# A 2-D Fourier mixer that adds x(t,e) and x(-t,-e) before its transforms instead of after them

## The chip, the cores and the metric

One core of a Trainium2 chip runs the whole kernel. The metric is the device time of one execution in microseconds, the median of the runs shown. The profile is of one execution; its times are microseconds from the start of its span. TensorE (PE) does the matmuls and the transposes, VectorE (DVE) and ScalarE (ACT) the elementwise work, GpSimd (POOL) next to nothing, and SyncE (SP) issues most of the DMAs.

## The reference

Two batches of 3136 tokens with 256 features go through an attention with squared ReLU, a low-rank token mixer with a first two-layer channel mixer, and then the stage that is changed here:

```python
def _moe2_ref(x, w_ch1, w_ch2) -> np.ndarray:
    X = np.fft.fft(x, axis=1)
    X = np.fft.fft(X, axis=2)
    mixed = np.real(X).astype(np.float32)
    u = x + mixed
    mu = np.mean(u, axis=-1, keepdims=True)
    var = np.mean((u - mu) ** 2, axis=-1, keepdims=True)
    un = (u - mu) / np.sqrt(var + 1e-06)
    ch = np.maximum(un @ w_ch1, 0.0) @ w_ch2
    return (u + ch).astype(np.float32)
```

The real part of the 2-D transform of x is what is wanted, for tokens (axis 1) and features (axis 2).

## The kernel before

The tokens are ordered so that the transform over 3136 = 64 x 49 tokens splits into one over 49 and one over 64, and so that negating a token index swaps neighbours (r) and moves whole stretches. Everything is float32; each factor of most matmuls is split into a high and a low part, so that a product is three matmuls.

After the attention comes one loop (the last of `program`) over the 28 chunks of the two channel mixers: two layers x two batches x seven chunks of 448 tokens. A chunk has eight hidden blocks, so the loop has 224 steps. Step i issues `hidden(i)` (six matmuls, then ReLU `Hh` on ScalarE, L323, and the low part `Hl` on VectorE, L324), then `project(i - 2)` (six matmuls into `psC`); the last project of a chunk ends in `finish` (two additions into `xT`, L353, in the first layer; two multiplications and two additions, L366 and L368, in the second). Then each generator in the list `active` issues one piece. `prep` of the next chunk is put at the head of the list at the third step of a chunk (k == 2); the others stand behind it in the order in which they were started: `tail` at step 3, `weights(0)` at 20, `fourier(0)` at 43, `fourier(1)` at 99, `weights(1)` at 104. The two Fourier generators rest at the first step of each chunk (k == 0). The schedule is manual: each engine gets its instructions in the order in which the program issues them, and waits are set where data need them.

`fourier(b)` works on `xT[b]`, which holds the features on the partitions (two halves, a = 0 and 1) and the tokens in the free dimension. `tokens(i)` transposes two stretches of 98 tokens, both halves, into one PSUM tile (four transposes, L768), and splits the result into `nh` (ScalarE) and `nl` (VectorE). `axis49(i - 1)` does the 49-point transform (three matmuls of 512 columns, L779 to L781), copies it to `wst` and stores it in DRAM (`scr`). That is 17 steps. `fetch` reads `scr` back, rearranged, as `wr`; after four steps `axis64` takes two of the 25 frequencies at a time, for each a matmul with both feature halves (L808), which yields the sums and differences of features e and -e. `features` then does the transform over the features (nine matmuls, L830 to L838) and adds its outputs to `xT` at both places. Feature 128 has no partner and is carried by a small side path (`er`, `feature128`, `row`).

`misc()` hands out three PSUM tiles (`m`, `x`, `g`) in turn. Helpers record their own line: ScalarE's copies are L92, VectorE's subtractions L95.

Of the kernel before, what the change touches and what calls it, by code (L numbers as in the profile page):

```python
# [10 lines left out]
F32 = mybir.dt.float32  # L11
# [16 lines left out]
def _orders():  # L28
    """Token order: position sl * 98 + i2 * 2 + r, with i1 = 2 * sl + r, holds the s with
    s = m1 (mod 64), s = m2 (mod 49), where m1 = o1[i1], m2 = o2[i2].  # L30

    o1 pairs each value with its negative, o2 runs 0..24, then -1..-24, so that a negation
    swaps r and moves whole stretches. Feature order: 0..127, then 128, -1, -2, .., -127.
    """
    o1 = np.array([0, 32] + [x for i in range(1, 32) for x in (i, 64 - i)])
    o2 = np.array(list(range(25)) + [49 - i for i in range(1, 25)])
    c1, c2 = pow(49, -1, 64), pow(64, -1, 49)
    tok = (49 * c1 * o1.reshape(32, 1, 2) + 64 * c2 * o2.reshape(1, 49, 1)) % S
    tok = tok.reshape(-1)
    feat = np.array(list(range(128)) + [128] + [256 - e for e in range(1, 128)])  # L40
    return o1, o2, c1, c2, tok, feat


def _constants():
    """DFT matrices (shapes alone): the 49-point and 64-point axes and the 256 features."""
    o1, o2, c1, c2, tok, feat = _orders()
    b49 = np.zeros((98, 128))
    t2 = 2 * np.pi * ((c2 * np.outer(o2, np.arange(KPOS))) % 49) / 49
    for par in range(2):
        b49[par::2, par * 32 : par * 32 + KPOS] = np.cos(t2)  # L50
        b49[par::2, 64 + par * 32 + 1 : 64 + par * 32 + KPOS] = np.sin(t2[:, 1:])
    t1 = 2 * np.pi * ((c1 * np.outer(o1, o1)) % 64) / 64
    f64 = np.block([[np.cos(t1), np.sin(t1)], [-np.sin(t1), np.cos(t1)]])
    row = np.array([2 * sl + par for par in range(2) for sl in range(32)])
    f64 = f64[np.concatenate([row, 64 + row])]
    e = np.arange(128)
    td = 2 * np.pi * (np.outer(e, e) % 256) / 256
    sign = np.zeros((128, 256))
    sign[:, 0] = 1.0 - 2.0 * (e % 2)
    sign[:2, 128:] = -2.0 * (e % 2)  # L60
    fd = np.concatenate([np.cos(td), np.sin(td), sign], axis=1)
    rep = np.tile(np.eye(32), (2, 4))
    mask = np.ones((128, 6))
    mask[:, 1] = mask[:, 2] = -1.0
    mask[0, :3] = [0.0, 0.0, 1.0]
    mask[:, 3] = 1e-6
    mask[:, 4] = -14336.0 * 2**19
    return {
        "b49": b49.astype(np.float32),
        "f64": f64.astype(np.float32),  # L70
        "fd": fd.astype(np.float32),
        "rep": rep.astype(np.float32),
        "mask": mask.astype(np.float32),
    }
# [7 lines left out]
def program(ctx, tc, zT, v, uT, U, V, w1a, w2a, w1b, w2b, b49, f64, fd, rep, mask, out):  # L82
# [34 lines left out]
    scr = [dram.tile([128, 32, D], F32, tag=f"scr{b}", name=f"scr{b}") for b in range(NB)]  # L117
# [4 lines left out]
    # constants  # L122
# [5 lines left out]
    f64s = [const.tile([128, 128], F32, name=f"f64s{a}") for a in range(2)]  # L128
# [3 lines left out]
    ones = const.tile([128, 128], F32R, name="ones")  # L132
    Utail = const.tile([128, 4, 64], F32R, name="Utail")
    Gs = [const.tile([128, D], F32R, name=f"Gs{b}") for b in range(NB)]

    def constants():
        make_identity(nc, ident)
        load(out=repc, in_=rep)
        load(out=maskc, in_=mask)
        t = ptile()  # L140
        load(out=t[0:98, 0:128], in_=b49)
        load(out=f64s[0], in_=f64)
        load(out=t[:, 256:768], in_=fd)
        nc.vector.memset(t[:, 768:896], 1.0 / D)
        yield
        yield
        hcopy(ones, t[:, 768:896])
        hcopy(b49h, t[0:98, 0:128])
        sub(b49l, t[0:98, 0:128], f(b49h))
        for dst, k in ((fA, 256), (fB, 384)):  # L150
            hcopy(dst[:, 0], t[:, k : k + 128])
            sub(dst[:, 1], t[:, k : k + 128], f(dst[:, 0]))
        hcopy(fN, t[:, 512:768].rearrange("p (a n) -> p a n", a=2))
        # the second half of the features: sines negated
        hcopy(f64s[1][:, 0:64], f64s[0][:, 0:64])
        nc.scalar.mul(f64s[1][:, 64:128], f64s[0][:, 64:128], -1.0)

    # float64 inputs arrive as their words
    def words(raw, np_, n):
        """float32 (the nearest) of the n float64 per partition at the start of raw."""  # L160
# [17 lines left out]
    # weights, in four tiles of 256 hidden units: [128, 2 (high, low), 2, 256], where the  # L178
    # third axis is the half of the features (first layer) or of the hidden units (second)
    class Weights:  # L180
# [3 lines left out]
        def split(self, k, y):  # L184
            """y: an eighth, [128, 256]"""
            part, q = divmod(k, 2)
            if q == 0:
                self.t[part] = self.pool.tile([128, 2, 2, 256], F32R, tag="w", name="w")
            w = self.t[part]
            if self.second:  # L190
                dst = w[:, :, q]
            else:
                y = y.rearrange("p (a n) -> p a n", a=2)
                dst = w[:, :, :, q * 128 : q * 128 + 128]
            hcopy(dst[:, 0], y)
            sub(dst[:, 1], y, f(dst[:, 0]))
# [15 lines left out]
    # the low-rank mixer: G = U^T a, accumulated over the tokens  # L212
# [11 lines left out]
    class Chunk:  # L224
# [33 lines left out]
        def prep2(self):  # L258
# [29 lines left out]
            # the variances: a row, then tokens 4 p + j on partition p  # L288
# [39 lines left out]
        def project(self, k):  # L328
# [5 lines left out]
            if self is chunks[-1] and k >= 6:  # L334
                # the first half of the features before the second, at the very end
# [38 lines left out]
    def attention(stack):  # L374
# [61 lines left out]
        # float64 inputs, piece by piece  # L436
# [31 lines left out]
        def conv_w(src, k, second, dst):  # L468
# [13 lines left out]
            if not second:  # L482
# [7 lines left out]
                # without its mean over the features: the norm's mean is gone with it  # L490
# [25 lines left out]
        def scores(b, qc, p):  # L516
# [13 lines left out]
            # the first one in halves: its products wait for it  # L530
# [33 lines left out]
        def gate(b, qc, last):  # L564
            """Two chunks share a tile: seven whole tiles of tokens for the mixer."""
# [11 lines left out]
        def groups(qc):  # L577
            """The tiles of 128 tokens (the last one has 64) that are worked on together."""
# [4 lines left out]
        def mix(b, qc, tiles, last):  # L583
            """The tiles' transposes."""
# [21 lines left out]
        def mix2(b, qc, tiles, h, l, n, last):  # L606
            """Their part of G."""
# [34 lines left out]
        # the engines' first instructions, before the data are there  # L642
# [116 lines left out]
    def fourier(b):  # L759
        """x <- x + Re(FFT2(x)) in place; yields between pieces of work."""  # L760
        nat, W = {}, {}

        def tokens(i):
            ps = misc()
            for s in range(2):
                for a in range(2):
                    src = xT[b][:, a, (2 * i + s) * 98 : (2 * i + s) * 98 + 98]
                    nc.tensor.transpose(  # L768
                        ps[0:98, s * D + a * 128 : s * D + a * 128 + 128], src, ident
                    )  # L770
# [5 lines left out]
        def axis49(i):  # L776
            h, l = nat.pop(i)
            ps = misc()
            mm(ps, b49h, h, start=True, stop=False)  # L779
            mm(ps, b49h, l, start=False, stop=False)  # L780
            mm(ps, b49l, h, start=False, stop=True)  # L781
            w = mp.tile([128, 512], F32, tag="wst", name="wst")
            hcopy(w, ps)
            load(out=scr[b][:, 2 * i : 2 * i + 2, :], in_=w.rearrange("p (s d) -> p s d", s=2))

        for i in range(17):
            if i < 16:
                tokens(i)
            if i > 0:
                axis49(i - 1)  # L790
            yield
# [3 lines left out]
        def fetch(g):  # L795
            n = min(2, KPOS - 2 * g)
            raw = W[g] = mp.tile([128, 2, D], F32, tag="wr", name="wr", bufs=3)
# [3 lines left out]
        def axis64(g, first, Th, Tl):  # L801
            """Two of the first 25 frequencies: the features' sums (cosine) and differences (sine)."""
# [3 lines left out]
            for j in range(n):  # L806
                for a in range(2):
                    mm(ps[:, j * 128 : j * 128 + 128], w[:, j, a * 128 : a * 128 + 128], f64s[a],  # L808
                       start=a == 0, stop=a == 1)
# [6 lines left out]
        # feature 128, which the folding of the features leaves on the wrong row  # L816
        e = mp.tile([128, KPOS], F32, tag="er", name="er", bufs=1)
        ch, cl = (mp.tile([KPOS, 64], F32R, tag=t, name=t, bufs=1) for t in ("ech", "ecl"))

        def feature128():  # L820
            ps = misc()
            mm(ps[0:KPOS, 0:64], e, f64s[0][:, 0:64], start=True, stop=True)
# [3 lines left out]
        def features(first, n, Th, Tl, row):  # L826
# [17 lines left out]
            # mneg is -1 except in row 0; sg is -1 except +1 in row 0  # L844
# [26 lines left out]
        for g in range(3):  # L871
            fetch(g)
            if g == 0:
                for c in range(4):
                    load(out=e[c * 32 : c * 32 + 32, :], in_=src[c, :, 0:KPOS, 128])
        for _ in range(4):
            yield
        late_adds = None
        for pairs in (range(0, 3), range(3, 6), range(6, 9), range(9, 13)):
# [3 lines left out]
            for g in pairs:  # L883
# [5 lines left out]
                if g == pairs[-1]:  # L889
                    # the high and the low part of feature 128, one row each  # L890
# [29 lines left out]
    with tc.manual_schedule():  # L920
# [3 lines left out]
            3: tail(), 20: weights(0), 43: fourier(0), 99: fourier(1), 13 * 8: weights(1),  # L924
        }
        calm = [starts[43], starts[99]]
# [31 lines left out]
def _host_layout(inputs):  # L958
# [15 lines left out]
    # the words of a float64 array, as the program reads them  # L974
# [23 lines left out]
```

## Time and profile before

| | |
|---|---|
| time, median of 3 runs | 1248.96 us (1248.58 to 1249.58) |
| span of the profiled execution | 1246.6 us |
| TensorE busy | 1239.5 us, 99% |
| VectorE busy | 814.2 us, 65% |
| ScalarE busy | 656.8 us, 53% |
| granted TensorE clock, mean | 1.000 |

The span runs from the first to the last instruction of the profiled execution. The profile has no separate total for that execution; the median of the runs is 2.4 us above the span, which is what lies around the instructions. The busy time of TensorE counts matmuls, whose ends are modelled and overlap. In the timeline rows a line is start, duration, engine, source line, operation, the tile written and the tiles read, and, in brackets, how long the engine had been idle and what it waited for.

### The profile page before, as it was taken

The page shows a single profiled execution, that of the slowest core. Times are in us where ns is not written, and L with a number is a line of the kernel's source. Part 1 is how long each engine was busy: PE and PEld are TensorE (multiplying, and loading weights), DVE is VectorE, ACT ScalarE, POOL GpSimd, SP SyncE. Part 2 cuts the span into 40 slices and gives each one's busy share as a digit, 9 for nine tenths or more (in the row PEclk, how much of TensorE's full clock was granted, in tenths as well). Part 3 has the DMA queues.
Part 4 walks back from the last instruction along what each step waited for, and adds up shares of the span by engine and source line. Part 5 has one row for each costly group of instructions (what it writes and reads, how often), then busy time and mean ns, then how long its engine had stood idle before and what let it go on. Part 6 is the DMA issues. An engine that isn't in the chain of part 4 may idle for free.

```text
span 1246.6 us, 16808 instructions
## 1 busy us (share of the span) xinstructions
PE 1239.5 (99%) x6270; PEld 1127.9 (90%) x6270; DVE 814.2 (65%) x1492; ACT 656.8 (53%) x1054; POOL 46.2 (4%) x90
## 2 busy tenths in 40 slices
PE   9999999999999999999999999999999999999998
PEld 7999999999899999999889988999989999999997
DVE  7867777988667566755555554567566677556564
ACT  7766676877566566666333354333465344343432
POOL 0000000000000000000000000000000111000100
PEclk9999999999999999999999999999999999999999
DMA  5311221334012112200221132321033221111111
GB/s 154 96 34 56 66 63 49 99 106 121 8 55 63 38 48 66 80 29 28 60 58 44 32 105 94 70 72 50 26 102 91 74 53 30 38 31 38 30 38 45
DMA packets 67297, 76.00 MB, mean 61 GB/s; under 512 B 18254, under 2 KB 60272, under 8 KB 67216
## 3 DMA queue, kind: packets, MB, share of 16 engines
q1 hardware_dynamic: 62752, 68.55, 18.3%
q0 software_dynamic: 4384, 6.27, 2.8%
q8 instruction: 49, 0.80, 0.3%
q14 instruction: 32, 0.26, 0.1%
q10 hardware_dynamic: 80, 0.11, 0.0%
HBM read 48.12 MB, written 23.76 MB: 58 GB/s over the span
## 4 chain that ended last, share of the span: by engine, by line
PE 96%; DVE 1%; ACT 1%; DMA 1%; issue 0%; SPq 0%; DVEq 0%; ACTq 0%
PE psO L560 11%; PE psO L557 11%; PE psO L559 11%; PE psH L318 7%; PE psC L343 7%; PE psC L345 7%; PE psH L319 7%; PE psC L344 7%; PE psH L320 7%; PE psS L527 6%; PE psS L528 6%; PE ps_g L612 1%; PE ps_m L593 1%; PE ps_m L808 1%; PE ps_x L808 1%; PE ps_g L808 1%
## 5 line engine op out<-in xcount | busy, mean ns | idle before, releaser
L324 DVE SCALAR_TENSOR_TENSOR Hl<-psH,Hh 128x448 fp32r<-128x448 f32 x224 | 139.7, 624 | 181.5 <-ACT Hh L323 181.4
L557 PE MATMUL psO<-h,Vt 128*128 128x448 f32 x700 | 256.5, 366 | 0.1
L560 PE MATMUL psO<-h,Vt 128*128 128x448 f32 x700 | 256.5, 366 | 0.0
L323 ACT ACTIVATE Hh<-psH 128x448 fp32r<-128x448 f32 x224 | 122.1, 545 | 245.2 <-PE psH L320 240.6
L559 PE MATMUL psO<-l,Vt 128*128 128x448 f32 x672 | 246.3, 366 | 0.4 <-DVE l L95 0.4
L533 ACT ACTIVATE P<-psS 128x896 f32<-128x896 f32 (+1 forms) x183 | 161.8, 885 | 149.1 <-PE psS L528 148.7
L95 DVE TENSOR_TENSOR l<-P,h 128x896 fp32r<-128x896 f32 (+1 forms) x197 | 201.2, 1021 | 23.5 <-ACT h L92 17.7
L537 DVE CAST h<-P 128x896 fp32r<-128x896 f32 (+1 forms) x183 | 111.0, 607 | 148.9 <-ACT P L536 147.6
L536 ACT ACTIVATE P<-P 128x896 f32<-128x896 f32 (+1 forms) x183 | 168.5, 921 | 5.7
L318 PE MATMUL psH<-h,w 128*128 128x448 f32 x448 | 166.6, 372 | 0.0
L319 PE MATMUL psH<-l,w 128*128 128x448 f32 x448 | 164.0, 366 | 0.2 <-DVE l L95 0.2
L343 PE MATMUL psC<-Hh,w 128*128 128x448 f32 x448 | 164.0, 366 | 0.0
L345 PE MATMUL psC<-Hh,w 128*128 128x448 f32 x448 | 163.9, 366 | 0.0
L344 PE MATMUL psC<-Hl,w 128*128 128x448 f32 x448 | 163.6, 365 | 0.0
L320 PE MATMUL psH<-h,w 128*128 128x448 f32 x448 | 163.4, 365 | 0.0
L560 PEld LDWEIGHTS psO<-h,Vt 128*128 128x128 f32 x700 | 131.5, 188 | 11.9 <-DVE Vt L95 0.5
L557 PEld LDWEIGHTS psO<-h,Vt 128*128 128x128 f32 x700 | 131.4, 188 | 11.9 <-DVE aT L572 0.4
L559 PEld LDWEIGHTS psO<-l,Vt 128*128 128x128 f32 x672 | 126.2, 188 | 11.8 <-DVE l L95 0.9
L527 PE MATMUL psS<-T 128*128 128x448 f32 x336 | 125.1, 372 | 0.3 <-DVE T L95 0.2
L528 PE MATMUL psS<-T,T 128*128 128x448 f32 x336 | 123.5, 367 | 0.0
L318 PEld LDWEIGHTS psH<-h,w 128*128 128x128 f32 x448 | 84.2, 188 | 9.6 <-issue 0.5
L319 PEld LDWEIGHTS psH<-l,w 128*128 128x128 f32 x448 | 84.3, 188 | 7.6 <-DVE l L95 0.5
(276 smaller groups left out, 1482.1 us busy)
## 6 DMA issues: line engine op xcount, KB each, us to landing
scr<-wst SPq DMA_DIRECT2D x32, 256.0 KB, 2.0
uT<-in_uT SPq DMA_DIRECT2D x14, 448.0 KB, 4.0
vraw<-in_v SPq DMA_DIRECT2D x24, 256.0 KB, 2.8
wr<-scr SPq DMA_DIRECT2D x96, 64.0 KB, 2.0
out<-P SPq DMA_DIRECT2D x27, 224.0 KB, 2.0
aTd<-aT SPq DMA_DIRECT2D x13, 448.0 KB, 2.9
P<-aTd SPq DMA_DIRECT2D x13, 448.0 KB, 4.0
Vr<-Vd SPq DMA_DIRECT2D x56, 56.0 KB, 3.1
```

Source lines behind the costliest of these rows:

```text
L95: tt(out=o, in0=a, in1=b, op=ALU.subtract)
L318: mm(ps[:, 0:CH], wh, self.h[:, a], start=a == 0, stop=False)
L319: mm(ps[:, 0:CH], wh, self.l[:, a], start=False, stop=False)
L320: mm(ps[:, 0:CH], wl, self.h[:, a], start=False, stop=a == 1)
L343: mm(dst, wh, h, start=k == 0, stop=False)
L344: mm(dst, wh, l, start=False, stop=False)
L345: mm(dst, wl, h, start=False, stop=k == 7)
L527: mm(ps[:, j, 0:CH], k, q1, start=True, stop=False)
L528: mm(ps[:, j, 0:CH], k, q2, start=False, stop=True)
L557: mm(dst, vh, hj, start=p == 0 and j == 0, stop=False)
L559: mm(dst, vh, lj, start=False, stop=False)
L560: mm(dst, vl, hj, start=False, stop=p == 12)
```

## The change

The four ways to take (t,e) and (-t,-e) are joined at the start. A new function `fold` adds, on VectorE, the first half of the features and the second half at the negated token into a tile `y` of 128 features by four stretches of 98 tokens. `tokens(i)` calls it and then transposes the four stretches of `y`; there are 8 such pieces per batch instead of 16. `axis49` stores four stretches at a time, with 128 columns per token. `fetch` and `axis64` work with 128 columns per token, one matmul per frequency. Feature 128 comes out of `xT` by a DMA of its own into `raw128` and goes through transpose, split, 49-point transform and a VectorE transpose in a new piece, `column128`; the eight loads of `er` go. `features` is as it was. The starts of the two Fourier generators move from 43 and 99 to 50 and 106, and the pause ahead of `axis64` has six steps instead of four. The rest of the diff takes out comments.

```diff
@@ -114,32 +114,34 @@
...
-    scr = [dram.tile([128, 32, D], F32, tag=f"scr{b}", name=f"scr{b}") for b in range(NB)]
+    scr = [dram.tile([128, 32, 128], F32, tag=f"scr{b}", name=f"scr{b}") for b in range(NB)]
...
-    f64s = [const.tile([128, 128], F32, name=f"f64s{a}") for a in range(2)]
+    f64s = const.tile([128, 128], F32, name="f64s")
...
+    raw128 = const.tile([128, 98], F32, name="raw128")
...
+        nc.gpsimd.memset(raw128, 0.0)
...
-        load(out=f64s[0], in_=f64)
+        load(out=f64s, in_=f64)
...
@@ -757,35 +756,74 @@
     late["small"] = small
 
     def fourier(b):
         nat, W = {}, {}
+        x0, x1 = (xT[b][:, a].rearrange("p (s m r) -> p s m r", m=49, r=2) for a in range(2))
+        def fold(y, s0, s1):
+            yv = y.rearrange("p (s m r) -> p s m r", m=49, r=2)
+            for t0, t1 in ((0, 1), (1, s1)) if s0 == 0 else ((s0, s1),):
+                for m, w in ((0, 0), (1, 25), (25, 1)):
+                    n = 24 if m else 1
+                    in1 = x1[:, t0:t1, w : w + n]
+                    if t0:
+                        in1 = in1[:, :, :, ::-1]
+                    tt(
+                        out=yv[:, t0 - s0 : t1 - s0, m : m + n],
+                        in0=x0[:, t0:t1, m : m + n],
+                        in1=in1,
+                        op=ALU.add,
+                    )
 
         def tokens(i):
+            y = mp.tile([128, 392], F32, tag="y", name="y")
+            fold(y, 4 * i, 4 * i + 4)
             ps = misc()
-            for s in range(2):
-                for a in range(2):
-                    src = xT[b][:, a, (2 * i + s) * 98 : (2 * i + s) * 98 + 98]
-                    nc.tensor.transpose(
-                        ps[0:98, s * D + a * 128 : s * D + a * 128 + 128], src, ident
-                    )
+            for s in range(4):
+                nc.tensor.transpose(ps[0:98, s * 128 : s * 128 + 128], y[:, s * 98 : s * 98 + 98], ident)
             h, l = (t[0:98] for t in pair_late())
             hcopy(h, ps[0:98, :])
             sub(l, ps[0:98, :], f(h))
             nat[i] = (h, l)
 
-        def axis49(i):
-            h, l = nat.pop(i)
-            ps = misc()
+        def dft49(ps, h, l):
             mm(ps, b49h, h, start=True, stop=False)
             mm(ps, b49h, l, start=False, stop=False)
             mm(ps, b49l, h, start=False, stop=True)
+        def axis49(i):
+            ps = misc()
+            dft49(ps, *nat.pop(i))
             w = mp.tile([128, 512], F32, tag="wst", name="wst")
             hcopy(w, ps)
-            load(out=scr[b][:, 2 * i : 2 * i + 2, :], in_=w.rearrange("p (s d) -> p s d", s=2))
-        for i in range(17):
-            if i < 16:
+            load(out=scr[b][:, 4 * i : 4 * i + 4, :], in_=w.rearrange("p (s d) -> p s d", s=4))
+        e = mp.tile([128, 32], F32, tag="er", name="er", bufs=1)
+        def column128():
+            ps = misc()
+            nc.tensor.transpose(ps[0:98, 0:128], raw128, ident)
+            h, l = (t[0:98, 0:32] for t in pair_late())
+            hcopy(h, ps[0:98, 0:32])
+            sub(l, ps[0:98, 0:32], f(h))
+            ps = misc()
+            dft49(ps[:, 0:32], h, l)
+            w = mp.tile([128, 512], F32, tag="wst", name="wst")[:, 0:32]
+            hcopy(w, ps[:, 0:32])
+            nc.vector.transpose(out=e, in_=w)
+        for i in range(9):
+            if i < 8:
                 tokens(i)
+            if i == 7:
+                load(out=raw128[0:32, :], in_=xT[b][0:1, 1, :].rearrange("o (s p) -> o s p", p=98))
             if i > 0:
                 axis49(i - 1)
             yield
@@ -794,32 +832,28 @@
 
         def fetch(g):
             n = min(2, KPOS - 2 * g)
-            raw = W[g] = mp.tile([128, 2, D], F32, tag="wr", name="wr", bufs=3)
+            raw = W[g] = mp.tile([128, 2, 128], F32, tag="wr", name="wr", bufs=3)
             for c in range(4):
                 load(out=raw[c * 32 : c * 32 + 32, 0:n, :], in_=src[c, :, 2 * g : 2 * g + n, :])
 
         def axis64(g, first, Th, Tl):
             w = W.pop(g)
             n = min(2, KPOS - 2 * g)
             ps = misc()
             for j in range(n):
-                for a in range(2):
-                    mm(ps[:, j * 128 : j * 128 + 128], w[:, j, a * 128 : a * 128 + 128], f64s[a],
-                       start=a == 0, stop=a == 1)
+                mm(ps[:, j * 128 : j * 128 + 128], w[:, j, :], f64s, start=True, stop=True)
             pv = ps[:, 0 : n * 128].rearrange("p (k c n) -> p c k n", k=n, c=2)
             o = (2 * g - first) * 64
             th, tl = (x[:, :, o : o + n * 64].rearrange("p c (k n) -> p c k n", n=64) for x in (Th, Tl))
             hcopy(th, pv)
             sub(tl, pv, f(th))
 
-        e = mp.tile([128, KPOS], F32, tag="er", name="er", bufs=1)
         ch, cl = (mp.tile([KPOS, 64], F32R, tag=t, name=t, bufs=1) for t in ("ech", "ecl"))
 
         def feature128():
             ps = misc()
-            mm(ps[0:KPOS, 0:64], e, f64s[0][:, 0:64], start=True, stop=True)
+            mm(ps[0:KPOS, 0:64], e[:, 0:KPOS], f64s[:, 0:64], start=True, stop=True)
             hcopy(ch, ps[0:KPOS, 0:64])
             sub(cl, ps[0:KPOS, 0:64], f(ch))
 
@@ -870,10 +904,9 @@
 
         for g in range(3):
             fetch(g)
-            if g == 0:
-                for c in range(4):
-                    load(out=e[c * 32 : c * 32 + 32, :], in_=src[c, :, 0:KPOS, 128])
-        for _ in range(4):
+        for i in range(6):
+            if i == 4:
+                column128()
             yield
         late_adds = None
         for pairs in (range(0, 3), range(3, 6), range(6, 9), range(9, 13)):
@@ -921,9 +954,9 @@
         nstep = len(chunks) * 8
         active = []
         starts = {
-            3: tail(), 20: weights(0), 43: fourier(0), 99: fourier(1), 13 * 8: weights(1),
+            3: tail(), 20: weights(0), 50: fourier(0), 106: fourier(1), 13 * 8: weights(1),
         }
-        calm = [starts[43], starts[99]]
+        calm = [starts[50], starts[106]]
         for i in range(nstep + 2):
             c, k = divmod(i, 8)
             if i < nstep:
```

## Rows read from the trace of the kernel before

**Rows 1.** The page, section 1: busy time, share of the span, instructions.
```profile
PE 1239.5 (99%) x6270; PEld 1127.9 (90%) x6270; DVE 814.2 (65%) x1492; ACT 656.8 (53%) x1054; POOL 46.2 (4%) x90
```

**Rows 2.** Windows: stretch, length, busy us by engine (instructions), granted clock, DMA.
```profile
748.12:751.73 3.61, 3.61 (x20) 3.20 (x19) 1.32 (x3) 1.72 (x3) 0.00 (x0) 1.00 0.30 111
755.31:757.74 2.43, 2.43 (x13) 2.20 (x12) 0.63 (x2) 0.55 (x1) 0.00 (x0) 1.00 0.05 13
785.42:788.66 3.24, 3.24 (x22) 3.06 (x20) 2.05 (x4) 0.55 (x1) 0.00 (x0) 1.00 0.17 47
```

**Rows 3.** Timeline, step 54: start, duration in us, engine, line, operation.
```profile
747.67 0.62 DVE L324 SCALAR_TENSOR_TENSOR Hl<-psH,Hh 128x448 fp32r<-128x448 f32 x1 [0.47 <-ACT Hh L323]
748.12 0.60 PE L768 MATMUL ps_x<-ident,xT 128*98 128x128 f32 x4
```

**Rows 4.** Timeline, step 52: prep's product and VectorE's work.
```profile
740.75 0.60 PE L768 MATMUL ps_g<-ident,xT 128*98 128x128 f32 x4
742.20 0.63 DVE L95 TENSOR_TENSOR l<-P,h 128x448 fp32r<-128x448 f32 x1 [0.63 <-ACT h L92]
742.74 0.69 DVE L95 TENSOR_TENSOR nl<-ps_g,nh 98x512 fp32r<-98x512 f32 x1
```

**Rows 5.** Groups by form on VectorE: count, busy us, mean ns.
```profile
L868 DVE TENSOR_TENSOR xT<-xT,A 128x186 f32<-128x186 f32 x16 | 7.4, 515 | 0.0
L172 DVE SCALAR_TENSOR_TENSOR stg<-stg 128x192 int32<-128x192 int32 x4 | 1.4, 352 | 0.0
```

**Rows 6.** Timeline, steps 57, 58 and 121: finish and Vs.
```profile
757.74 0.60 PE L768 MATMUL ps_g<-ident,xT 128*98 128x128 f32 x4
757.84 1.15 DVE L353 TENSOR_TENSOR xT<-psC,P 128x448 f32<-128x448 f32 x2
...
761.36 0.60 PE L768 MATMUL ps_x<-ident,xT 128*98 128x128 f32 x4
761.55 1.27 DVE L95 TENSOR_TENSOR Vs<-Vr,Vs 32x448 fp32r<-32x448 f32 x2
...
962.26 1.16 DVE L368 TENSOR_TENSOR P<-P,xT 128x448 f32<-128x448 f32 x2
```

**Rows 7.** Timeline, near 610 us: a matmul that waits for VectorE.
```profile
609.30 0.68 DVE L95 TENSOR_TENSOR nl<-ps_m,nh 128x512 fp32r<-128x512 f32 x1
610.04 0.47 PE L251 MATMUL ps_m<-Vs,Gs 128*128 128x448 f32 x1 [0.25 <-DVE nl L95]
...
612.78 0.37 PE L251 MATMUL ps_x<-Vs,Gs 128*128 128x448 f32 x1
```

**Rows 8.** Timeline, steps 106 and 108 to 111: TensorE's transposes, prep's last VectorE work.
```profile
910.65 0.60 PE L768 MATMUL ps_g<-ident,xT 128*98 128x128 f32 x4
912.00 0.63 DVE L95 TENSOR_TENSOR sm<-sm 128x448 fp32r<-128x448 f32 x1 [0.63 <-ACT sm L92]
913.28 0.43 DVE L95 TENSOR_TENSOR w<-wraw,w 128x256 fp32r<-128x256 f32 x1
...
918.24 0.60 PE L768 MATMUL ps_x<-ident,xT 128*98 128x128 f32 x4
918.44 1.15 DVE L95 TENSOR_TENSOR P<-xT,ps_m 128x448 f32<-128x448 f32 x2 [0.42 <-PE ps_m L270]
...
921.85 0.60 PE L768 MATMUL ps_m<-ident,xT 128*98 128x128 f32 x4
921.93 1.15 DVE L95 TENSOR_TENSOR l<-xT,h 128x448 fp32r<-128x448 f32 x2
...
925.42 0.60 PE L768 MATMUL ps_g<-ident,xT 128*98 128x128 f32 x4
925.91 0.63 DVE L283 TENSOR_TENSOR sm<-P 128x448 f32<-128x448 f32 x1 [0.31 <-ACT P L281]
...
928.99 0.60 PE L768 MATMUL ps_x<-ident,xT 128*98 128x128 f32 x4
929.09 0.62 DVE L95 TENSOR_TENSOR sm<-sm 128x448 fp32r<-128x448 f32 x1
```

More of the change, by code (lines that the diff above doesn't have):

```diff
@@ L153, in constants @@
         hcopy(fN, t[:, 512:768].rearrange("p (a n) -> p a n", a=2))
-        hcopy(f64s[1][:, 0:64], f64s[0][:, 0:64])
-        nc.scalar.mul(f64s[1][:, 64:128], f64s[0][:, 64:128], -1.0)
     def words(raw, np_, n):
```

## The prediction

> **What bounds the kernel now.** I read the page first, then the Fourier stage in windows, then single steps of it in the timeline. The page leaves one reading: TensorE is busy 99% of the span [rows 1], so a saving on it shortens the kernel and a wait on it lengthens it, and an engine other than TensorE matters only where TensorE stands behind it. [...]
>
> The Fourier mixer is woven into the main loop: pass i (a "step") issues hidden(i), project(i-2), then one piece each of the generators in the list: prep always first, then the others in the order in which they were started. A step without any Fourier work lasts 2.43 us, one with tokens and axis49 3.61, one with axis64 3.24 [rows 2]. So tokens with axis49 cost 1.18 us of TensorE, and axis64 on two frequencies 0.81 us; for that the row has 8 more matmuls than the 12 of the main loop, since each of the four float32 products runs as two passes, 0.101 us a pass. There is no idle time in these stretches: TensorE is busy for the whole of each.
>
> The next thing to see is where VectorE stands when TensorE comes to the transposes. In a step without prep (54) they start at 748.12, while VectorE finishes Hl of the same step at 748.29 (747.67 + 0.62) [rows 3]: VectorE trails by 0.17 us. That harms nobody, because these transposes read xT, which was ready long ago, and their results are used a step later. VectorE keeps to the order of issue: nl of the transposes comes behind the work of prep, never before it [rows 4].
>
> **The change, part by part.**
>
> *Removed from TensorE.* tokens and axis49 now cover four stretches of 98 tokens at a time with half the columns each: 8 pieces per batch for 16, with the same four transposes and three products of 512 columns in each. 16 pieces fewer in both batches x 1.18 = 18.9 us. axis64 runs one product per frequency for two: 25 x 2 batches x 2 passes = 100 passes x 0.101 = 10.1 us. Together 29.0 us. If TensorE alone counted the kernel would gain 2.3%.
>
> *Added: fold, and a wait.* Before each group of transposes VectorE now adds x(t,e) and x(-t,-e) into a new tile y, and the transposes of the same step load y as weights. fold is issued in the step where it is needed, behind everything that VectorE was given earlier in that step. So TensorE reaches the transposes and must wait for (a) what VectorE still has in front of fold, (b) fold, (c) the way back to TensorE. Behind the transposes stand axis49, and hidden and project of the next steps, so the whole wait is on the path.
>
> (b) fold is three additions: 8, 192 and 192 elements. 448 elements take 0.62 us, and 192 elements with one input read in steps of two elements take 0.352 us, so 1.05 ns an element on top of 0.15; 186 elements with inputs and output all in such steps take 0.515 us, 2 ns an element on the same 0.15 [rows 3, 5]. In fold only one input is out of order (pairs reversed) and the other operands are contiguous, which is nearest to the 0.352 row. Successive additions overlap by 0.08 to 0.1 us: two of 0.62 together last 1.15 [rows 6]. So fold adds 0.16 + 2 x 0.352 - 3 x 0.09 = 0.59 us to VectorE's queue; by the strided row, at 192 x 2 ns + 0.15 = 0.53 us each, 0.95. The lower bound is the elements alone, 392 x 1.05 ns = 0.41. The first fold of each batch has six additions, some 0.2 us more.
>
> The row says that stepping on both inputs and the output doubles the price, and that stepping on one input is free. [...]
>
> (c) From the end of an addition to a matmul that needs it: nl ends at 609.98, the weight load behind it starts at 610.04, and its matmul is recorded as 0.47 us long where the next one of its kind takes 0.37 [rows 7]: 0.06 + 0.10 = 0.16 us.
>
> (a) I read this for each step in which the new kernel runs tokens (50 to 55, 57, 58 for the first batch; 106 to 111, 113, 114 for the second; the generator rests at each eighth step), from a step of the old one at the same place of its chunk: end of the last VectorE work issued ahead of the Fourier generator, minus the start of the transposes.
>
> First batch: behind Hl alone 0.17 (three steps) [rows 3]; behind prep's product, addition, cast and l, 742.83 - 740.75 = 2.08 (two steps) [rows 4]; behind finish, 758.99 - 757.74 = 1.25 [rows 6]; behind the two Vs subtractions, 762.82 - 761.36 = 1.46 (two steps) [rows 6]. Sum 8.8 us.
>
> Second batch, where prep is the longer one of the second layer and weights(1), started at 104, is now ahead of fourier(1), started at 106, with its subtraction w (0.34 us behind other work) in seven of the eight steps. Step 106: sm ends at 912.63, w then at 912.97, against 910.65: 2.3 [rows 8]. Step 107: Hl and w: 0.6. Step 108: 919.59 - 918.24 + 0.34 = 1.7. Step 109: 923.08 - 921.85 + 0.34 = 1.6. Step 110: 926.54 - 925.42 + 0.34 = 1.5. Step 111: 929.71 - 928.99 + 0.34 = 1.1 [rows 8]. Step 113: finish and w, 1.25 + 0.34 = 1.6. Step 114: as 106 without w, 2.0. Sum 12.4 us.
>
> The waits add up to 8.8 + 12.4 + 16 x (0.59 + 0.16) + 0.4 = 33.6 us. What hides none of it: TensorE has no other work to take up, its order is fixed. What is late next: nothing beyond, since ACT and VectorE catch up in the wait.
>
> *Added: column128,* once per batch, in steps 65 and 121, right after finish: a transpose, a cast on ScalarE, a subtraction on VectorE, then three products of 32 columns, all in one step. The subtraction stands behind finish: 1.25 us in the first layer; in the second finish has two more additions, 1.16 us [rows 6], so 2.4. With a small subtraction (0.1 after overlap), the way back (0.16), and the short products (0.2 beyond what the wait covers), 1.7 and 2.9 us: 4.6 together. At the least, were the subtraction to be ready when the cast is, about 1.0 each.
>
> *Moved or covered.* The starts move from 43 and 99 to 50 and 106; with 8 pieces fewer and two more pauses axis64 begins in the same step as before (67 and 123), so features and everything behind them keep their places. The scr stores halve in number, the wr fetches halve in bytes with three groups in hand, and the eight small er loads give way to two raw128 loads, issued on SP seven steps (some 17 us) ahead of use: nothing, covered by that lead. Were it gone, TensorE would wait out the landing of one small DMA per batch. Two small ACT copies and a memset at the beginning stand beside attention's matmuls: nothing. In the axis64 steps TensorE shrinks by 0.4 us of 3.24, and VectorE, busy 2.05 us of such a step [rows 2], comes closer to being the bound; I take nothing, up to 3 us.
>
> **Sum.** 1246.6 - 18.9 - 10.1 + 33.6 + 4.6 = 1255.8 us of span. The median of the runs, 1248.96, stands 2.4 us above the span, so 1258.2. The bounds of its own: 392 elements alone per fold and the cheaper column128 take off 5 (1253); strided folds add 5.8, and VectorE's bound 3 (1267).
>
> **Rivals.**
>
> *The clock falls.* TensorE would be idle for about 3 us at a stretch in four steps (106, 114, and both prep steps of the first batch). The rows show the clock at 1.00 [rows 2], but none has such a gap, so they don't exclude a fall. [...]
>
> *fold ahead of the queue (the other side).* If the additions ran behind Hl alone, with 0.17 us in front in all 16 steps, the waits would be 16 x 0.92 + 0.4 = 15.1 and the time 1248.96 - 29.0 + 15.1 + 4.6 = 1240, faster. It decides where the mean of (a) falls under 0.75 us; I read 1.33. Against it: in each step above VectorE and ScalarE ran in the order of issue, even where a later instruction was ready.
>
> *Balance.* With the low bounds, and prep's chains a third shorter than read, the waits come to about 24 us and the time to 1248, no change.
>
> **How the numbers follow.** 0.2% (2.5 us) is what a measurement here tells from no change. My forecast has 0.79, the clock 0.09, fold ahead of the queue 0.07, balance 0.05: faster 0.07, same 0.05, slower 0.88. The range leaves out the faster case and the end of the clock's: 1250 to 1270.
>
> **What would show it.** Right: in a tokens step TensorE idle for 0.9 to 3.3 us before the weight load of y, released by VectorE's addition into y, 16 times and some 34 us in all; fold at about 0.35 us per large addition; two such waits for nl in column128; 100 passes of axis64 at 0.10 us; granted clock 1.00 throughout. Wrong: y finished before TensorE comes to it; or waits as read, but half-clock stretches behind them; or idle time in the axis64 steps.

## The result, and the profile after

The changed kernel takes 1263.33 us (median of 4 runs, 1259.22 to 1264.94) against 1248.77 (1248.39 to 1249.58) beside it: 1.0111 times as long, 95% interval 1.0093 to 1.0130. Slower by 14.6 us; 1258.2 was forecast, in a range of 1250 to 1270. The profiled execution took 1261.89 us, with a span of 1260.1 and a mean granted clock of 0.993.

Page, section 1 (answers to [rows 1]), TensorE's row of section 2, and the chain that ended last:

```profile
PE 1221.3 (97%) x6066; PEld 1108.9 (88%) x6066; DVE 813.0 (65%) x1534; ACT 639.6 (51%) x1024; POOL 45.9 (4%) x91
...
PE   9999999999999999999999968999878999999998
...
PE 94%; DVE 3%; ACT 1%; issue 1%; DMA 1%; SPq 0%; DVEq 0%; ACTq 0%
```

TensorE has less to do, 1221.3 us busy for 1239.5, and yet the span grew: 99% busy has become 97%. Each digit of the PE row is 31.5 us, and the ones below 9 are two groups: the 24th and 25th (724 to 788 us) and the 29th to 31st (882 to 976). These are the stretches in which the two batches go through `tokens`. VectorE now holds 3% of the chain, for 1% before.

The two ways in which a step waits, in the timeline. First step 52, with prep ahead (answers to [rows 4]), and step 54, without (answers to [rows 3]):

```profile
735.85 0.37 PE L250 MATMUL ps_x<-Vs,Gs 128*128 128x448 f32 x1
...
737.51 0.63 DVE L95 TENSOR_TENSOR l<-P,h 128x448 fp32r<-128x448 f32 x1 [0.63 <-ACT h L92]
738.05 0.70 DVE L777 TENSOR_TENSOR y<-xT 128x8 f32<-128x8 f32 x3
738.90 0.62 PE L789 MATMUL ps_g<-ident,y 128*98 128x128 f32 x4 [2.68 <-DVE y L777]
...
748.67 0.62 DVE L323 SCALAR_TENSOR_TENSOR Hl<-psH,Hh 128x448 fp32r<-128x448 f32 x1 [1.13 <-ACT Hh L322]
748.91 0.37 PE L344 MATMUL psC<-Hh,w 128*128 128x448 f32 x1
749.21 0.69 DVE L777 TENSOR_TENSOR y<-xT 128x8 f32<-128x8 f32 x3
749.96 0.64 PE L789 MATMUL ps_x<-ident,y 128*98 128x128 f32 x4 [0.69 <-DVE y L777]
```

The matmuls of 448 columns start 0.20 us apart where nothing is late (six from 734.84 to 735.85). In step 52 the transposes could start at 736.05 and start at 738.90: 2.85 us, through VectorE's l and then the three additions into y; 2.83 had been worked out (2.08 + 0.59 + 0.16). In step 54 they could start at 749.11 and start at 749.96: 0.85 us, or 0.89 when it is counted from the matmul behind the transposes (0.92 had been worked out). All 16 waits, each counted from that matmul, are 2.39, 0.87, 2.86, 2.85, 0.89, 0.96, 2.00, 2.32 in the first batch (15.1, forecast 15.0) and 3.35, 1.28, 2.46, 1.87, 2.22, 1.82, 2.39, 2.10 in the second (17.5, forecast 18.6): 32.6 us.

The additions by themselves, all instructions of the line (minimum, median and maximum in ns):

```profile
L777 DVE TENSOR_TENSOR y<-xT x54: 154/350/359, 727.6 to 954.1; 128x192 f32<-128x192 f32 x28, 128x8 f32<-128x8 f32 x14, 128x48 f32<-128x48 f32 x4, 128x144 f32<-128x144 f32 x4
```

`column128` of the second batch (step 121), and what follows it:

```profile
975.90 0.27 PE L812 MATMUL ps_m<-ident,raw 128*98 128x128 f32 x1
976.06 1.15 DVE L365 TENSOR_TENSOR P<-psC,rs 128x448 f32<-128x448 f32 x2
...
976.45 0.28 PE L796 MATMUL ps_x<-nh,b49h 98*128 98x32 f32 x1 [0.28 <-ACT nh L92]
977.12 1.15 DVE L367 TENSOR_TENSOR P<-P,xT 128x448 f32<-128x448 f32 x2
978.19 0.18 DVE L95 TENSOR_TENSOR nl<-ps_m,nh 98x32 fp32r<-98x32 f32 x1
978.43 0.28 PE L797 MATMUL ps_x<-nl,b49h 98*128 98x32 f32 x1 [1.69 <-DVE nl L95]
...
979.17 0.37 PE L319 MATMUL psH<-h,w 128*128 128x448 f32 x1
...
980.03 0.57 PE L319 MATMUL psH<-h,w 128*128 128x448 f32 x1
980.40 0.57 PE L342 MATMUL psC<-Hh,w 128*128 128x448 f32 x1
```

The subtraction nl stands behind the four additions of finish, and TensorE behind nl: from the transpose (975.90) to the first hidden matmul (L317; 978.76, counted back 0.20 us from the matmul behind it) 2.86 us, 1.72 in the first batch; 2.9 and 1.7 were forecast. The last two rows show something that the sum did not have: matmuls of 448 columns start 0.37 us apart and are 0.57 long, where they start 0.20 apart and are 0.36 long elsewhere. The granted clock is 0.50 there (980 to 982 us), and 1.00 just before (978.43 to 979.37).

Windows of 8 us around the places where it fell (columns as in [rows 2], the granted clock third from the end):

```profile
904.00:912.00 8.00, 5.43 (x22) 4.41 (x21) 3.95 (x12) 2.31 (x5) 0.00 (x0) 0.79 0.06 16
920.00:928.00 8.00, 5.97 (x24) 5.11 (x25) 3.56 (x9) 2.94 (x6) 0.00 (x0) 0.79 0.17 49
944.00:952.00 8.00, 5.78 (x23) 4.88 (x22) 3.99 (x11) 2.56 (x5) 0.14 (x1) 0.80 0.11 35
952.00:960.00 8.00, 6.08 (x24) 5.05 (x24) 3.15 (x8) 3.29 (x5) 0.00 (x0) 0.78 0.09 33
976.00:984.00 8.00, 6.03 (x24) 5.22 (x23) 4.37 (x10) 1.48 (x4) 0.00 (x0) 0.79 0.15 57
```

Five stretches, behind the waits of steps 106, 108, 113 and 114 and behind column128. In the first batch the clock stays at 1.00 (724 to 904 us), behind waits of 2.85 too.

So 1246.6 - 29.0 + 32.6 + 4.6 = 1254.8 us of span by the terms of the prediction with their measured waits, and 5.3 us are left, which the clock would have to explain (what the two traces differ by ahead of the stage comes under waits filled). Theory: the change saves 29 us, the waits for y and column128 take 37 of them, and the clock a few more. Rivals: the saving is smaller than counted; or it isn't the wait for VectorE's queue that costs, but the fold itself or the stage's new order.

### The profile page after: what moved, and what is told of

The parts are those of the page before. It is cut to its first block, busy times and chain, and to the rows that moved or that the text cites. A ratio compares the mean times of both kernels' runs of the same rounds, so it can differ in the third digit from the quotient of the medians.

```text
span 1260.1 us, 16361 instructions
## 1 busy us (share of the span) xinstructions
PE 1221.3 (97%) x6066; PEld 1108.9 (88%) x6066; DVE 813.0 (65%) x1534; ACT 639.6 (51%) x1024; POOL 45.9 (4%) x91
## 4 chain that ended last, share of the span: by engine, by line
PE 94%; DVE 3%; ACT 1%; issue 1%; DMA 1%; SPq 0%; DVEq 0%; ACTq 0%
PE psO L559 11%; PE psO L556 11%; PE psO L558 11%; PE psH L317 7%; PE psH L318 7%; PE psH L319 7%; PE psC L342 7%; PE psC L343 7%; PE psC L344 7%; PE psS L526 6%; PE psS L527 6%; PE ps_g L611 1%; DVE y L777 1%; PE ps_m L592 1%; ACT Hh L322 1%
## 5 line engine op out<-in xcount | busy, mean ns | idle before, releaser
L317 PE MATMUL psH<-h,w 128*128 128x448 f32 x448 | 168.2, 375 | 0.0
L317 PEld LDWEIGHTS psH<-h,w 128*128 128x128 f32 x448 | 85.2, 190 | 9.6 <-issue 0.5
```

Of the source, the lines that this page charges most:

```text
L317: mm(ps[:, 0:CH], wh, self.h[:, a], start=a == 0, stop=False)
```

## The experiments

**fold ahead.** The additions are issued one step before the transposes that need them, behind the previous step's transposes; one step of the pause ahead of `axis64` goes, so that `axis64` begins as before.

```diff
         def tokens(i):
-            y = mp.tile([128, 392], F32, tag="y", name="y")
-            fold(y, 4 * i, 4 * i + 4)
+            y = ys.pop(i)
...
-        for i in range(9):
-            if i < 8:
+        ys = {}
+        for i in range(-1, 9):
+            if 0 <= i < 8:
                 tokens(i)
-            if i == 7:
+            if i + 1 < 8:
+                y = ys[i + 1] = mp.tile([128, 392], F32, tag="y", name="y")
+                fold(y, 4 * i + 4, 4 * i + 8)
+            if i == 6:
...
-        for i in range(6):
-            if i == 4:
+        for i in range(5):
+            if i == 3:
                 column128()
```

> Each fold is issued one step ahead of its transposes (the tokens pieces start one step later, the pause before axis64 is one step shorter); the work is the same. If the 34 us of waits for y are what the change costs, and the falls of the clock come from them, both go: 1248.8 - 29.0 + 4.6 (column128 stays) = about 1224 us, clock 1.00 but for a fall near column128 of the second batch. If VectorE's added work itself were the cost, wherever it stands in the queue, the time would stay above 1245 us.

Measured: 1223.19 us (1222.78 to 1224.25), 0.9801 of the kernel before (0.9785 to 0.9817), 40 us under the changed kernel. Step 54 in its timeline:

```profile
738.23 0.62 DVE L323 SCALAR_TENSOR_TENSOR Hl<-psH,Hh 128x448 fp32r<-128x448 f32 x1
738.39 0.36 PE L344 MATMUL psC<-Hh,w 128*128 128x448 f32 x1
738.59 0.60 PE L788 MATMUL ps_g<-ident,y 128*98 128x128 f32 x4
...
740.51 0.69 DVE L777 TENSOR_TENSOR y<-xT 128x8 f32<-128x8 f32 x3
```

The transposes start 0.20 us after the last project matmul, with no wait in brackets, though VectorE is still at Hl; the additions at 740.51 are those of the next step, whose transposes come at 742.17. All waits for y together are 0.7 us, and the clock is 0.999. The same additions, as long as before (median 348 ns), cost 33 us in one place and under 1 us in the other: it is the queue. Of the 40 us some 32 are these waits; the rest goes with the clock (7.1 us in waits filled).

**fold and column ahead.** On top of that, `column128` is split and moved ahead of finish: the transposition, cast and subtraction run in steps 62 and 118, the products in 63 and 119, where all of it was in 65 and 121.

```diff
             sub(l, ps[0:98, 0:32], f(h))
+            yield
             ps = misc()
             dft49(ps[:, 0:32], h, l)
...
+        col = column128()
+        for i in range(5):
+            if i in (1, 2):
+                next(col, None)
             yield
```

> As the kernel with fold one step ahead, and column128 in two steps: transpose and split in one, the 49-point products in the next, both before the step of finish. The theory of waits takes another 4 us off, about 1220.5 us, with no fall of the clock. If column128's price were its matmuls and not its wait, it would stay at 1224 us.

Measured: 1219.22 us (1217.35 to 1220.79), 0.9766 (0.9751 to 0.9780). This is the version that beats both kernels, by 29 us and by 44. Window of the whole stage:

```profile
720.00:1024.00 304.00, 303.73 (x1559) 275.56 (x1558) 206.07 (x459) 124.30 (x256) 15.80 (x30) 1.00 0.17 52
```

TensorE has no gap left to speak of, 303.73 of 304 us, and VectorE has room, 206. The 4.0 us below the version before are near the 4.6 of column128; the matmuls of its own stay and lengthen steps 63, 64, 119 and 120 by 0.8 us together. Whether the split was needed, or moving it ahead of finish would have done, was not tried.

**waits filled.** The changed kernel, with matmuls that nobody needs ahead of the transposes, as many as fit each wait (5 to 23 of 256 columns, into the PSUM tile that the transposes then overwrite), and 8 and 16 in `column128`.

```diff
+FILL0 = (17, 5, 21, 21, 5, 5, 14, 17)
+FILL1 = (23, 9, 18, 16, 16, 12, 17, 19)
...
             ps = misc()
+            for _ in range((FILL0, FILL1)[b][i]):
+                mm(ps[:, 0:256], ones, fA.rearrange("p a n -> p (a n)"), start=True, stop=True)
             for s in range(4):
...
             ps = misc()
+            for _ in range((8, 16)[b]):
+                mm(ps[:, 0:256], ones, fA.rearrange("p a n -> p (a n)"), start=True, stop=True)
             dft49(ps[:, 0:32], h, l)
```

> The changed kernel with idle TensorE time filled: before each group of transposes, and before column128's products, matmuls of constants (256 columns, 0.11 us each) write the PSUM tile that is then overwritten, by count somewhat less than the wait read in the trace of the changed kernel. They give no result that is used. If the falls of the clock cost some 6 to 7 us, they go and the time falls to about 1256 us at clock 1.000, with less spread. If they cost nothing, or come for another reason, the time stays at 1261 to 1265 us or rises.

Measured: 1256.18 us (1254.93 to 1257.33), 1.0062 (1.0047 to 1.0077), span 1255.6. The first and the last of the windows above:

```profile
904.00:912.00 8.00, 7.83 (x51) 7.29 (x50) 4.76 (x14) 2.54 (x5) 0.00 (x0) 1.00 0.05 16
...
976.00:984.00 8.00, 8.00 (x44) 7.48 (x43) 3.75 (x8) 2.75 (x6) 0.00 (x0) 1.00 0.16 54
```

The clock is 1.00 there and, in the mean, over the whole span, and the kernel is 7.1 us faster than the changed one although TensorE does more. The order of the work and VectorE's part in the waits are the same, so what is gone is the falls of the clock. The two profiled spans differ by 4.5 us, but the traces differ ahead of the stage already: step 44 begins at 708.32 in the changed kernel's and at 710.54 here. From there to the end they take 551.8 and 545.0 us, 6.8 less here: 0.2 up to the start of step 99 (885.64 and 887.63), in the first batch, where the clock never fell, and 6.6 behind it, where the five stretches lie, some 1.3 us a fall.

The five executions of the changed kernel on record show the same: spans of 1257.4, 1260.1, 1261.7, 1263.2 and 1263.0 us at mean clocks of 0.995, 0.993, 0.991, 0.990 and 0.989.

**after again.** The changed kernel once more, with a profile.

> The changed kernel as it is, for a second trace. Waits for y of 32 to 33 us in all, as in the first. On the clock: if a fall hangs on the length of a wait alone, it comes behind the same five waits again (after steps 106, 108, 113, 114, 121) and behind none of the first batch; if something else decides, the falls stand behind other waits, in other number, and the time differs by some 1.5 us a fall.

Measured: 1263.50 us, span 1261.7, waits for y 33.7 us. Windows, and the transposes of step 52:

```profile
736.00:744.00 8.00, 5.46 (x16) 4.83 (x17) 2.72 (x7) 2.28 (x4) 0.00 (x0) 0.63 0.20 48
744.00:752.00 8.00, 5.32 (x18) 4.36 (x17) 2.92 (x7) 1.74 (x3) 0.00 (x0) 0.73 0.24 83
...
912.00:920.00 8.00, 6.56 (x27) 5.42 (x28) 3.59 (x12) 2.51 (x5) 0.00 (x0) 0.79 0.05 16
920.00:928.00 8.00, 5.71 (x26) 4.84 (x25) 3.53 (x9) 2.10 (x5) 0.00 (x0) 0.86 0.23 79
...
944.00:952.00 8.00, 5.78 (x31) 4.87 (x31) 4.38 (x10) 2.80 (x6) 0.58 (x1) 1.00 0.10 33
952.00:960.00 8.00, 5.40 (x29) 4.57 (x29) 3.78 (x8) 3.46 (x6) 0.00 (x0) 1.00 0.10 34
...
976.00:984.00 8.00, 6.03 (x24) 5.09 (x23) 3.64 (x9) 1.46 (x4) 0.54 (x1) 0.79 0.16 58
...
738.54 1.06 PE L789 MATMUL ps_g<-ident,y 128*98 128x128 f32 x4 [2.68 <-DVE y L777]
```

Five stretches again. Three lie at the same places as before: at step 106, whose transposes come at 912.29 here, at 908.17 there, behind step 108 (924.59) and behind column128. Two lie elsewhere: steps 113 and 114, which fell there, don't fall here, and steps 52 and 53 do. Step 52 had 2.68 us without a matmul in both traces; here its four transposes take 1.06 us and the granted clock is 0.50 behind them (740 to 744 us), there they take 0.62, at 1.00. The length of a wait alone doesn't decide.

**fold twice.** The changed kernel with the additions done twice.

```diff
-            fold(y, 4 * i, 4 * i + 4)
+            for _ in range(2):
+                fold(y, 4 * i, 4 * i + 4)
```

> The changed kernel (1263.3 us) with every fold done twice in the same place. The theory of waits puts each microsecond of fold on the path: 16 x 0.59 + 0.4 = 9.8 us more, 1273 us, and up to 1277 if the longer waits bring more falls of the clock. If fold were largely hidden behind something else that TensorE waits for, it would stay within 3 us of 1263.

Measured: 1278.27 us (1276.18 to 1280.89), 1.0239 (1.0221 to 1.0257). The waits for y grew from 32.6 to 41.1 us, 0.53 a piece. That understates it, since behind a stretch of low clock TensorE itself comes late to the transposes (in the changed kernel step 114 waits 2.10 us behind one and 2.78 without). In steps 55, 57 and 58, with the clock at 1.00, the waits are 1.57, 2.62 and 2.93 for 0.96, 2.00 and 2.32, 0.61 a piece, where 0.59 had been taken. In step 57 TensorE is idle for 2.42 us ahead of the transposes, for 1.80 in the changed kernel:

```profile
769.34 0.65 PE L790 MATMUL ps_g<-ident,y 128*98 128x128 f32 x4 [2.42 <-DVE y L777]
```

At that price the folds make some 10 of the 14.9 us. The rest goes with a mean clock of 0.979 for 0.993 in the profiled executions; that was not tried by itself.

**ahead, fold twice.** The same doubling in the version with fold and column ahead.

> The kernel with fold and column128 ahead (1219.2 us), again with every fold done twice: the same 9.8 us of added VectorE work as in the run before, but with a step's time for it. By the theory of waits it costs nothing, 1219 to 1221 us. If VectorE's load cost time by itself, 1225 us or more.

Measured: 1222.74 us (1221.54 to 1224.12), 0.9794 (0.9779 to 0.9808): 3.5 us above that version, 1.7 above the top of what was expected. A step ahead hides one fold nearly whole (0.7 us of waits), two not everywhere (4.6). The end of step 107, whose transposes need the additions issued in step 106:

```profile
893.88 0.37 PE L344 MATMUL psC<-Hh,w 128*128 128x448 f32 x1
893.88 1.72 DVE L777 TENSOR_TENSOR y<-xT 128x2 f32<-128x2 f32 x12
895.15 0.32 PE L788 MATMUL ps_x<-ident,y 128*98 128x128 f32 x1 [0.90 <-DVE y L777]
```

Prep's chain of step 106 still stands ahead of the additions, which start only when TensorE comes to its last project matmul of step 107. There one step is just long enough for that chain and a single fold (0.68 us of wait without the doubling).

**Fourier first.** In each step the Fourier generators issue their piece before prep and weights, and everything else is as in the changed kernel.

```diff
-            for g in list(active):
+            for g in sorted(active, key=lambda g: g not in calm):
```

> The changed kernel with one thing else: in each step the Fourier generator issues its piece ahead of prep and weights. So fold stands behind Hl alone (0.17 us), and behind finish in two steps; fold itself and the way back stay. By the prediction's parts: waits 14 x 0.92 + 2 x 2.0 + 0.4 = 17.3 us, so 1248.8 - 29.0 + 17.3 + 4.6 = about 1242 us, if the clock does not fall; two or three falls would give 1245. If the queue ahead of fold was not the larger part of the waits, the time stays at 1255 us or more.

Measured: 1251.78 us (1249.21 to 1254.27, 9 runs), 1.0022 (1.0012 to 1.0033), 7 us above the upper of the two expected times (1242 without falls of the clock, 1245 with some). Its trace shows where it missed. In the timeline step 51, then a product of `features` and one of prep:

```profile
731.00 1.27 DVE L95 TENSOR_TENSOR Vs<-Vr,Vs 32x448 fp32r<-32x448 f32 x2
...
732.30 0.62 DVE L323 SCALAR_TENSOR_TENSOR Hl<-psH,Hh 128x448 fp32r<-128x448 f32 x1
732.84 0.69 DVE L777 TENSOR_TENSOR y<-xT 128x8 f32<-128x8 f32 x3
733.59 0.64 PE L789 MATMUL ps_g<-ident,y 128*98 128x128 f32 x4 [1.53 <-DVE y L777]
...
985.61 0.41 PE L867 MATMUL ps_x<-row,fN 2*128 2x384 f32 x1 [1.23 <-DMA row<-ecl]
...
990.87 0.36 PE L290 MATMUL ps_m<-sm,ones 128*1 128x448 f32 x1 [1.13 <-DVE sm L95]
```

The fold now precedes prep's work of its own step, but the Vs of the step before pushes Hl back, and the fold behind it: 1.74 us in place of 0.92, 2.44 in step 107; the waits for y are 21.1 us, not 17.3. Behind that come waits of TensorE that were not in the sum: 1.3 us for a DMA of `row` (step 127) and 1.3 for prep's sm (step 128); steps 92, 136 and 148 are 1.7 us longer as well. And the clock fell, in the windows

```profile
904.00:912.00 8.00, 5.76 (x28) 4.91 (x27) 4.44 (x10) 3.38 (x7) 0.00 (x0) 0.90 0.03 10
912.00:920.00 8.00, 7.07 (x34) 5.83 (x33) 4.56 (x12) 2.56 (x5) 0.00 (x0) 0.89 0.27 88
960.00:968.00 8.00, 6.03 (x25) 5.16 (x24) 3.06 (x7) 1.43 (x4) 0.54 (x1) 0.81 0.16 58
```

by up to 8 x (0.10 + 0.11 + 0.19) = 3.2 us. Together 3.8 + 2.6 + 1.7 + up to 3.2 = up to 11.3, for 9.8 between 1251.78 and 1242; none of them was tried by itself.

**axis64 twice.** On the version with fold and column ahead, each product of `axis64` done twice, which puts the 100 passes back.

```diff
-                mm(ps[:, j * 128 : j * 128 + 128], w[:, j, :], f64s, start=True, stop=True)
+                for _ in range(2):
+                    mm(ps[:, j * 128 : j * 128 + 128], w[:, j, :], f64s, start=True, stop=True)
```

> The kernel with fold and column128 ahead (1219.2 us), with each matmul of axis64 issued twice in a row into the same place, 100 passes more. It prices the second of the two savings: by the prediction's 0.101 us a pass, 10.1 us more, 1229 us. If the removed products had been partly hidden behind their weight loads or behind VectorE, it would be under 1225 us.

Measured: 1230.40 us (1229.69 to 1232.38), 11.2 above that version, where 10.1 was the term. The passes are worth 0.112 us each rather than 0.101: step 67, one with axis64, lasts 3.24 us in the trace of the kernel before, 2.79 in that of the changed one and 3.24 again here.

## Why the prediction was right

**What bounds the kernel** held: a saving on TensorE came out whole as soon as nothing stood in its way (29.2 us in fold and column ahead), and a wait on TensorE cost its length (31.9 us of waits for y, with some 7 of clock, in the 40.1 by which fold ahead is faster).

**The saving**, 29.0 us, is shown: fold and column ahead is 29.2 us below the kernel before by the medians. Of that, 1.7 us in the traces lie ahead of the stage (step 43 begins at 707.16 before, at 705.46 there); from step 43 to the end it takes 511.7 us for 539.4, which is 27.7, and with the 0.7 us of waits that are left and the 0.8 of column128's own matmuls the saving itself is again 29.2. Inside the term two errors cancel, which is luck: axis64's passes were priced too low (11.2 for 10.1), and a piece of tokens too high, since 18.0 us are left for 16 of them, where 18.9 was taken (step 46 lasts 3.61 us with a piece and 2.48 without, 1.13 for 1.18). The rival of a smaller saving falls.

**The waits for y**, 33.6 us, measured 32.6. (a) The queue ahead of the fold, read from steps of the kernel before at the same place of their chunk, held to 0.1 us in the first batch. In the second two steps came out shorter, 109 (1.87 for 2.35) and 114 (2.10 for 2.75), and the queue is not the reason: a stretch of low clock lies ahead of both (0.79 from 920 to 928 us, 0.80 from 944 to 952), so TensorE came late and waited less. From the matmul behind step 113's transposes to the last project matmul of step 114 it took 4.57 us; in the second trace, with no fall between them, 3.02, and step 114 waits 2.78 there. The chain of step 106 (starts, durations, what), the longest of them, is what (a), (b) and (c) look like in a row:

```profile
905.06 0.62 DVE Hl L323
905.68 0.54 DVE sm L262
...
906.25 0.57 ACT sm L92
...
907.39 0.42 DVE w L95
907.81 0.83 DVE y L777 x6
...
908.68 0.88 PE ps_x L789 x3
```

TensorE's last project matmul starts at 905.30; the end of w, 907.81, stands 2.3 us behind the place where the transposes could start, as [rows 8] had it. That the queue is the cause is shown by fold ahead: the same additions one step earlier, and 32 of the 33 us are gone.

**(b) The fold** was taken at 0.352 us per large addition from the row with one input in steps [rows 5], against 0.53 from the strided one. It is 0.350, the median of the line; the 28 additions of 192 elements, all with pairs in reversed order, take 352 ns in the mean. The strided row had been misread: in L868 of the kernel before the output and one input step by 98 elements, not by two, and only the other input by two. That changes nothing in the sum. fold twice gives 0.61 us per fold in TensorE's waits, at full clock.

**column128**: 1.72 and 2.86 us for 1.7 and 2.9. Splitting it and moving it ahead of finish gave 4.0 us back.

**Covered edits**: the loads of `raw128`, the stores and fetches hold up TensorE nowhere in the changed kernel (from 700 to 1245 us it waits for y, nl and nh alone), and `axis64` steps kept TensorE busy, so VectorE's bound (up to 3 us) did not come.

**The clock** is the term that was mis-sized: 0 in the sum, "the granted clock 1.00 throughout" in what would show it right, and half-clock stretches behind the waits among the signs of being wrong. On this point the prediction was wrong: the falls cost about 7 us (waits filled), with five stretches of low clock in each of two traces (0.50 inside those of the first). As a rival a fall had been named in four steps, with 9 chances in 100. How much it would cost no run had shown; in the runs it is some 1.3 us a fall. The chance was too low, and the steps are partly others: 106 fell in both traces, 114 in the first only, both prep steps of the first batch in the second only, 113 in the first only, and 108 and column128, which the rival left out like 113, in both. Why a given wait brings a fall in one execution and not in another stays open.

**The time** came out 5.1 us above the forecast and not 7. By the traces a part of that is luck: the changed kernel's reaches step 44 at 708.32, that of the kernel before at 709.96, and this start lies anywhere from 705.66 to 710.54 in the ten traces, though the code ahead of it is all but the same. Also, time and span of one execution differ by about 1.8 us on record (1261.89 and 1260.1), where 2.4 was added.

**The other rivals.** Fold ahead of the queue did not happen by itself; VectorE kept the order of issue (in step 52 the additions start at 738.05, behind l at 737.51), and only an edit of that order brought it. It was priced at 1240 with the step's own Hl in front; Fourier first came near that order and reached 1251.78, because work that is moved behind the fold lands in front of the next one.

## What to carry to other kernels

Where a saving on the busiest engine is paid for with an operation on another one, ask where in that engine's queue the new operation stands: 16 times 0.6 us of additions cost 33 us at the end of the queue and under 1 us one step earlier. The price can be read from the kernel before, as the end of the other engine's last work minus the time at which the busy engine arrives. Where a change is paid for in waits of TensorE, put its clock into the sum as a term of its own, not as a far rival: here it fell at idle times of 1.69 to 2.68 us, five times in each of two traces, to 0.50 inside those of the first, and that cost about 7 us.

## What the runs showed of the hardware that was not expected

The clock fell at idle times of TensorE of 1.69 to 2.68 us in the two traces of the changed kernel, and not by their length alone: 2.68 us in step 52 left it at 1.00 in one execution (738.90 to 741.00) and at 0.50 in another (740 to 744). Part of what a fall costs comes back in the next wait, which TensorE reaches late (step 114: 2.10 us behind a fall, 2.78 without). Behind column128 it fell although the windows from 960 to 976 us were busy throughout (8.00 of 8.00), and it fell only after matmuls had resumed: the clock was 1.00 from 978.43 to 979.37, then some nine matmuls of 448 columns started 0.37 us apart instead of 0.20, at 0.50. Filling the waits with matmuls that nobody needs made the kernel 7.1 us faster. An addition of 192 elements that reads pairs in reversed order took VectorE 352 ns in the mean, as much as one with a read in steps of two [rows 5].
